# Tok2 steps between the halves of a channel unit, and the score rounds of batch 1 from its second head quad on in twos

## The chip, the cores and the metric

The kernel runs on one core of a Trainium2 chip. The metric is the device time of one execution in microseconds; the time before is 375.89 us, the median of six executions (374.99 to 380.59). All times below are microseconds unless marked otherwise. In the profile PE is TensorE (matmuls), PEld its weight loads, DVE VectorE, ACT ScalarE, POOL GpSimd, and SP SyncE, which here only issues transfers.

## What is computed

Sigmoid attention over 8 batches of 12 heads, 448 positions and 64 channels a head, and then one MLP-mixer block (token mixing over positions, channel mixing over the 768 features):

```python
scores = scale * q @ k.T - log(S)            # per batch and head, S = 448
attn   = 1 / (1 + exp(-scores))
x      = (attn @ v)  laid out as (8, 448, 768)
h      = relu(x.T @ w_tok1) @ w_tok2         # 448 -> 256 -> 448, per batch
u      = x + h.T
h2     = relu(u @ w_ch1) @ w_ch2             # 768 -> 1536 -> 768
out    = u + h2
```

All matmuls of the kernel are in fp16 with fp32 sums; inputs and output are fp32.

## The kernel before

Every piece of work is an `Op`: a name, an engine, an estimated duration, what must come before it, the buffers it uses, and a function that emits its instructions. `Plan.run` plays the whole kernel through by these estimates before anything is emitted: for each engine it picks the next operation, and where TensorE is free it asks `choose`. The operations are then emitted in the order of the planned starts. On the chip each engine works through its own list in that order, and waits where something that it needs is not there yet. So an edit of `choose` can move any step of the kernel, and with it the order on the other engines.

The steps of TensorE, with their names (b is the batch, m one of three head quads, four heads each):

- `S_b_m_i` is a score round, i = 0 to 6: four 64x64 matmuls of 448 columns that run side by side in the four quarters of the array (L578). It fills one of two score buffers in PSUM (`wide`). ScalarE then makes the sigmoid of it (`sig`, L594), which frees the buffer.
- `V_b_m` is the value step of a quad: 28 matmuls of 64x64 (L616) into two PSUM banks; ScalarE reads them out (`xT`, L653), and the result is laid back into `X` by a transpose on TensorE (`B_b_m`, L675) or, in most batches from 2 on, by a DMA transpose from SP (`x_b_m_s`, L664).
- `K1_b` (tok1, L817 and L857) and `K2_b_blk_half` (tok2, L933) are the two token matmuls. For batches 2 to 7 a part of them runs as 64x64 matmuls (`V1_b_t`, L841, and `V2_b`, L891; the code calls these tails). After tok2, VectorE forms u = x + h (L955, L923), ScalarE casts it to fp16 (L963), and it is turned into `uT`, by SP (`uT_b_blk`, L991) or, for the last two blocks of batches 1 and 2, on TensorE (`U_b_blk`, L976).
- `C1_b_cb` (channel 1, L1007, twelve units a batch) and `C2_b_blk_half` (channel 2, L1066, six or eight units) are the channel matmuls, 128x128. Each unit is planned in two halves, the second named with `_h`: 3 + 3 matmuls in a channel-1 unit, 6 + 6 in a channel-2 unit. Both halves sum into one PSUM bank; VectorE reads it out at the end (L1023 for channel 1, L1079 for channel 2).

There are four such banks (`bank`), shared by all steps but the scores. The loads of q, k and v come from POOL's queue and are held back by small copies on POOL (`gate`, L781), each of which waits for a sigmoid three head quads earlier. From batch 2 on k and q are permuted on POOL (L496) and transposed by SP (`turnk`, `turnq`, L501). SP also stores the results (`st_b_blk`, L1050 and L1044). SP's list is worked through in order, so a transfer that is not ready holds those behind it.

Score rounds come in `groups`, which are issued as one choice. For batch 1 each round is a group by itself (`parts`), with its three value steps as groups between them; from batch 2 on two rounds make a group, at times with a value step. `due` says from how much done mixer work on a group is due: -1 for batches 0 and 1 (always), and for later ones by LEAD and SPAN. `choose` collects the candidates that could start, keeps those within 0.06 us of the first, and takes the lowest priority number p:

- a due group has p = 1, one that is not due 5;
- tok1 and tok2 have 2, channel 1 has 3, channel 2 has 4;
- the first tok2 of a pair has 4.5 as long as less than REST of other mixer work was done since the last tok2; tok2 of batch 0 has 3.5;
- the second half of a channel unit has 1.2.

Of the kernel before, what the change touches and what calls it, by code (L numbers as in the profile page):

```python
# [55 lines left out]
class Plan:  # L56
# [15 lines left out]
    def op(self, name, engine, us, emit, after=(), uses=(), rank=0.0):  # L72
        o = Op(name, engine, us, emit, after, uses, rank)
        self.ops.append(o)
        return o
# [56 lines left out]
    def run(self, choose):  # L132

        lists = {}
        for o in self.ops:
            if o.engine != "PE":
                lists.setdefault(o.engine, []).append(o)
        free = dict.fromkeys([*lists, "PE", "POOL"], 0.7)
        free["POOL"] = 0.8
        mode = [None]  # L140
        self.left = len(self.ops)
        while self.left:
            best = None
            for e, ops in lists.items():
                if e == "LD":
                    ops = ops[:1]
                for o in ops:
                    r = self.ready(o)
                    if r is None:
                        continue  # L150
                    at = free[e]
                    if e == "LD":
                        at = max(free["POOL"], self.landed[-8])
                    key = (max(r, at), o.rank, r)
                    if best is None or key < best[0]:
                        best = (key, e, o)
            pick = choose(self, free["PE"])
            if pick is not None:
                t, ops, kind = pick
                if best is None or t <= best[0][0]:  # L160
                    for o in ops:
                        r = self.ready(o)
                        t = max(t, r, free["PE"])
                        if kind != mode[0]:
                            t += 0.1
                            mode[0] = kind
                        self.hold(o)
                        o.start, o.end = t, t + o.us
                        free["PE"] = t = o.end
                        self.log.append(o)  # L170
                        self.left -= 1
                    continue
            if best is None:
                raise RuntimeError(
                    "\n".join(
                        f"{o.name} <- {[d.name for d in o.after if d.end is None]}"
                        for o in self.ops
                        if o.start is None
                    )[:1500]
                )  # L180
            (t, _, _), e, o = best
            self.hold(o)
            o.start = t
            if e == "LD":
                far = self.load_far if self.pipe > 50.0 else 0.4
                free["POOL"] = t + o.n * o.issue
                self.pipe = max(self.pipe, free["POOL"] + 1.3) + o.us
                while self.hitch and self.pipe > self.hitch[0][0]:
                    self.pipe += self.hitch.pop(0)[1]
                o.end = self.pipe + far  # L190
                self.landed += [o.end] * o.n
            elif e == "SP":
                free[e] = t + o.us
                o.end = t + self.far + min(5.0, max(0.0, self.pipe - t - 0.5))
            else:
                o.end = free[e] = t + o.us
            lists[e].remove(o)
            self.log.append(o)
            self.left -= 1
        self.log.sort(key=lambda o: o.start)  # L200
        for o in self.log:
            o.emit()
# [3 lines left out]
def kernel(  # L206
# [23 lines left out]
    DH = D // 2  # L230
    att_scale = 1.0 / math.sqrt(E)
    att_bias = -math.log(S)
    LEAD, SPAN, REST, LATE = 20.0, 0.86, 0.8, 0
    FILL, UP, SURE = 21.0, 7, 0.8
    PACK, PACK2 = range(2, 8), range(2, 8)
    JOIN, PULL, ALONE = 0.05, 3.0, 3.5
    PAUSE = 1.5

    assert (B, H, S, E) == (8, 12, 448, 64) and D == 768 and TT == 256 and CC == 1536
# [178 lines left out]
    for x in ("q", "k"):  # L418
        o = next(early[(0, x)])
# [52 lines left out]
    def filler():  # L472


        spot = bank(f"fill_{fill['n']}", [128, 256])

        def emit():
            nc.tensor.matmul(
                out=spot[:, :], lhsT=uT[0][:, 0, 0:128], rhs=uT[0][:, 0, 0:256], start=True, stop=True
            )  # L480

        fill["n"] += 1
        return op(f"fill_{fill['n']}", "PE", 0.11, emit, [up], [spot, uT[0]])
# [292 lines left out]
    for n, unit in enumerate(units[6:], 6):  # L776
        for what, i in (("k", 1), ("q", 3), ("v", 5)):
            sig, at = rounds_of[units[n - 3]][i]
# [4 lines left out]
            o = op(f"gate_{what}_{n}", "POOL", 0.1, gate, [sig], [at, mark], rank=-5)  # L783
# [325 lines left out]
    for b in range(B):  # L1109
        rs = [o for o in visits[b] if o.name[0] == "S"]  # L1110
        vs = [o for o in visits[b] if o.name[0] == "V"]
        if b == 0:
            groups += [(b, i, [o]) for i, o in enumerate(rs)]
        else:
            if b == 1:
                parts = [[o] for o in rs]
                parts[9].append(vs[0])
                parts[15].append(vs[1])
                parts = [[o] for g in parts for o in g] + [[vs[2]]]
                groups += [(b, i / len(parts), g) for i, g in enumerate(parts)]  # L1120
                continue
            if b == 2:
                line = [(c, i / 21, o) for c in range(2, B) for i, o in enumerate(o for o in visits[c] if o.name[0] == "S")]
                value = [o for c in range(2, B) for o in visits[c] if o.name[0] == "V"]
                for i in range(0, len(line), 2):
                    part = [o for _, _, o in line[i : i + 2]]
                    if value and i >= 7 * (len(line) // 7 - len(value)) + 7 + LATE:
                        part.append(value.pop(0))
                    groups.append((*line[i][:2], part))
                groups += [(B - 1, 1.0, [o]) for o in value]  # L1130
    mix = [sum(o.us for o in (*K[b], *C1[b], *C2[b])) for b in range(B)]
    base = [sum(mix[:b]) for b in range(B)]
    state = {"done": 0.0, "chosen": None, "rest": 9.0}

    def due(g):
        b, i, _ = g
        return -1.0 if b < 2 else base[b - 1] - LEAD + i * SPAN * mix[b - 1]

    def settle():
# [6 lines left out]
        if any(o.name[:3] == "V2_" for o in c[2]):  # L1146
            state["rest"] = -PAUSE
        if row is not groups and c[2][0].name[0] != "V":
# [4 lines left out]
    def choose(plan, t):  # L1153
        settle()
        tails[:] = [o for o in tails if o.start is None]
        g = groups[0] if groups else None
# [9 lines left out]
        if groups:  # L1166
            g = groups[0]
            r = plan.ready(*g[2])
            if r is not None:
# [6 lines left out]
                p = -1 if g[0] == 0 else 1 if state["done"] >= due(g) - (PULL if more else 0) else 5  # L1176
# [9 lines left out]
        for rank, kinds in ((2, K), (3, C1), (4, C2)):  # L1186
            n = 0
            for row in kinds:
                for o in row:
                    if o.name[:2] == "K2" and o.name[-1] == "1" and row.index(o) > 0 and row[row.index(o) - 1].name[:-1] == o.name[:-1]:  # L1190
                        n += 1
                        continue
                    r = plan.ready(o)
                    if short and rank == 2:
                        r = None
                    if r is not None:
                        p = 4.5 if o.name[:2] == "K2" and o.name[-1] == "0" and state["rest"] < REST else rank
                        if o.name[:4] == "K2_0":
                            p = 3.5
                        if o.name[-2:] == "_h":  # L1200
                            p = 1.2
                        cands.append((max(r, t), p, [o], "128", row, o))
                    n += 1
                    if n > (3 if rank == 2 else 0):
                        break
                if n > (3 if rank == 2 else 0):
                    break
        o = fill.get("op")
# [5 lines left out]
        if 3.0 < t < FILL and (not cands or min(c[0] for c in cands) > t + 0.12) and up.start is not None:  # L1214
            if any(x <= t - SURE for x, _ in plan.free_slots("bank", up)):
                o = fill["op"] = filler()
# [11 lines left out]
    with tc.manual_schedule():  # L1228
        plan.run(choose)
# [30 lines left out]
```

## Time and profile before

| what | value |
|---|---|
| median of six executions | 375.89 us (374.99 to 380.59) |
| the profiled execution's own time | 374.99 us |
| its span, first to last instruction | 373.2 us |
| ScalarE sigmoids (L594) | 172, 987 ns each |
| channel 1 on TensorE (L1007) | 576 matmuls, 119.6 us busy |
| channel 2 on TensorE (L1066) | 672 matmuls, 117.1 us busy |
| scores (L578) and values (L616) on TensorE | 672 and 672 matmuls, 53.4 and 36.5 us busy |
| tok2 (L933) on TensorE | 104 matmuls, 21.6 us busy |
| transposes of u by SP (L991) | 24, 2.6 / 3.8 / 6.8 us to landing (least, median, most) |
| granted TensorE clock | 1.000 of full speed in the mean |

The page gives busy time for each engine as a share of the span, then the span in 40 slices with one digit each (the busy share in tenths). A timeline row has the start, the length, the engine, the line of the code, the operation and its count; "x4" means that four instructions in a row were merged. Matmuls overlap in the array, so their lengths are longer than the distance from one start to the next. Time in brackets at the end of a row is how long the engine had been idle, and what ended that.

### The profile page before, as it was taken

To read this page: it belongs to the slowest core of one execution; us is meant where nothing else is said; L and a number is where in the kernel's file an instruction comes from. 1 tells how busy PE (TensorE), PEld (TensorE's weight loads), DVE (VectorE), ACT (ScalarE), POOL (GpSimd) and SP (SyncE) were. 2 spreads that over 40 slices of the span, in tenths; PEclk is the share of its full clock that TensorE was granted. 3 is DMA by queue.
4 is the path that set the end of the run, shared out by engine and by line. 5 is a ranking of instruction groups with operands and counts; after the bars stand their busy time and mean duration, and the time that the engine had idled before them with its cause. 6 is when DMAs were issued, how large, how long until landed. Compare 5 with 4: busy or idle time off the path is not lost.

```text
span 373.2 us, 7967 instructions
## 1 busy us (share of the span) xinstructions
PE 365.0 (98%) x3188; PEld 186.3 (50%) x3188; DVE 175.5 (47%) x414; ACT 207.7 (56%) x269; POOL 115.4 (31%) x261
## 2 busy tenths in 40 slices
PE   8999999999999999999899999999999999999995
PEld 4455445554444544455444545444455555555653
DVE  4467336643424544343244454754462257665221
ACT  5996992377777767788567576845655121100000
POOL 8883326343453435444443343430000000000000
PEclk9999999999999999999999999999999999999999
DMA  6999999599999999999999899993104463300344
GB/s 101 180 185 206 210 209 180 115 186 191 120 138 141 198 159 126 131 137 191 205 182 133 127 185 198 166 160 73 30 2 113 95 135 87 74 0 2 84 103 110
DMA packets 97013, 50.06 MB, mean 134 GB/s; under 512 B 70544, under 2 KB 93456, under 8 KB 96976
## 3 DMA queue, kind: packets, MB, share of 16 engines
q0 software_dynamic: 24080, 21.62, 41.6%
q1 hardware_dynamic: 72656, 27.62, 41.5%
q8 instruction: 25, 0.41, 0.5%
q10 hardware_dynamic: 240, 0.31, 0.2%
q14 instruction: 12, 0.10, 0.1%
HBM read 43.45 MB, written 11.01 MB: 146 GB/s over the span
## 4 chain that ended last, share of the span: by engine, by line
PE 94%; DVE 1%; DMA 1%; ACT 1%; issue 0%; ACTq 0%
PE c L1007 30%; PE c L1066 29%; PE qk L578 11%; PE xa L616 8%; PE yn L933 5%; PE k L857 3%; DMA uT<-u 1%; PE tq L524 1%; PE tk L524 1%; PE xb L675 1%; PE idle L463 1%; ACT attn L594 1%; PE k L817 1%; PE k L841 1%; PE k L707 1%; PE yt L891 1%
## 5 line engine op out<-in xcount | busy, mean ns | idle before, releaser
L594 ACT ACTIVATE attn<-qk,att_bias 128x896 f16<-128x896 f32 (+1 forms) x172 | 161.5, 987 | 59.9 <-PE qk L578 59.0
L1007 PE MATMUL c<-uT,w_ch 128*128 128x448 f16 x576 | 119.6, 353 | 1.2 <-DMA uT<-u 1.2
L1066 PE MATMUL c<-w_ch,h2aT 128*128 128x384 f16 x576 | 100.0, 326 | 0.0
L1023 DVE TENSOR_SCALAR h2aT<-c 128x384 f16<-128x384 f32 x96 | 53.5, 557 | 80.4 <-PE c L1007 80.3
L1007 PEld LDWEIGHTS <-w_ch 128*128 128x128 f16 x576 | 52.5, 98 | 58.2 <-issue 13.4
L1066 PEld LDWEIGHTS <-h2aT 128*128 128x128 f16 x576 | 54.8, 98 | 40.6 <-issue 5.9
L1079 DVE TENSOR_TENSOR u<-u,c 128x384 f32<-128x384 f32 x48 | 26.6, 554 | 67.5 <-PE c L1066 67.2
L578 PE MATMUL qk<-qT,kT 64*64 64x448 f16 x672 | 53.4, 363 | 1.2 <-ACT qT L547 0.5
L616 PE MATMUL xa<-attn,v 64*64 64x448 f16 x672 | 36.5, 350 | 0.0
L781 POOL COPY mark<-attn 1x1 f16<-1x1 f16 x54 | 9.6, 178 | 80.3 <-ACT attn L594 78.3
L963 ACT ACTIVATE u<-u 128x768 f16<-128x768 f32 x21 | 17.7, 843 | 28.9 <-DVE u L955 28.9
L578 PEld LDWEIGHTS <-kT 64*64 64x64 f16 x672 | 14.6, 104 | 32.4 <-issue 29.9
L496 POOL COPY kp<-k 128x384 f16<-128x384 f16 (+1 forms) x54 | 21.2, 429 | 19.0 <-DMA k<-in_k_dram 15.0
L955 DVE TENSOR_TENSOR u<-x,yn 128x384 f32<-128x384 f16 x48 | 24.6, 548 | 4.8 <-PE yn L933 4.7
L653 ACT ACTIVATE xT<-xa 128x448 f16<-128x448 f32 (+2 forms) x61 | 22.2, 440 | 7.2 <-PE xa L616 5.7
L616 PEld LDWEIGHTS <-v 64*64 64x64 f16 x672 | 19.5, 107 | 11.8 <-issue 0.7
L496 POOL COPY qp<-q 128x384 f16<-128x384 f16 (+1 forms) x54 | 21.3, 431 | 12.4 <-DMA q<-in_q_dram 12.4
L933 PE MATMUL yn<-h,w_tok 128*128 128x384 f16 x104 | 21.6, 327 | 0.0
L1023 DVE TENSOR_SCALAR h2odd<-c 128x64 f16<-128x64 f32 x96 | 20.5, 214 | 0.0
L340 POOL DMA_DIRECT2D q<-in_q_dram x21 | 15.0, 716 | 7.5 <-issue 5.8
L1066 PE MATMUL c<-w_ch,h2odd 128*128 128x384 f16 x96 | 17.1, 327 | 0.0
L340 POOL DMA_DIRECT2D k<-in_k_dram x21 | 15.1, 721 | 4.5 <-issue 4.5
(73 smaller groups left out, 205.9 us busy)
## 6 DMA issues: line engine op xcount, KB each, us to landing
out_dram<-u SPq DMA_DIRECT2D x48, 192.0 KB, 3.0
k<-in_k_dram POOLq DMA_DIRECT2D x21, 224.0 KB, 5.3
q<-in_q_dram POOLq DMA_DIRECT2D x21, 224.0 KB, 5.4
v<-in_v_dram POOLq DMA_DIRECT2D x21, 224.0 KB, 5.5
w_ch<-in_moe_w_ch_dram POOLq DMA_DIRECT2D x6, 768.0 KB, 18.5
out_dram<-ut SPq DMA_DIRECT2D x6, 192.0 KB, 3.6
v<-in_v_dram POOLq DMA_DIRECT2D x6, 112.0 KB, 5.5
x<-xT SPq DMA_TRANSPOSE x32, 4.2
```

Source lines behind the costliest of these rows:

```text
L340: nc.gpsimd.dma_start(out=t.ap().rearrange("r h j e -> r h (j e)"), in_=heads.rearrange("(h s) (p j) e -> (s p) h (j e)", s=2, j=J),)
L496: nc.gpsimd.tensor_copy(out=pm[:, to, :, :], in_=src[:, fr, :, :])
L578: nc.tensor.matmul(out=ps[64 * s : 64 * s + 64, h, 0:S], lhsT=kT[64 * h : 64 * h + 64, i, s, :], rhs=qT[64 * h : 64 * h + 64, :, s, :], st ...
L594: nc.scalar.activation(out=at[:, hs, :], in_=ps[:, hs, 0:S], func=SIGMOID, bias=bias_t[:, :], scale=att_scale,)
L616: nc.tensor.matmul(out=ps[s](slice(64 * h, 64 * h + 64)), lhsT=vf[64 * s : 64 * s + 64, h, order[i], :], rhs=attn[i][64 * s : 64 * s + 64, ...
L653: nc.scalar.activation(out=xt[:, s, to : to + n], in_=ps[s](every)[:, fr : fr + n], func=COPYF)
L933: nc.tensor.matmul(out=ps[:, :], lhsT=w_tok2[:, t, s0 : s0 + 2, :], rhs=h1[b][:, t, c], start=(t == 0), stop=(t == 1),)
L955: nc.vector.tensor_tensor(out=to, in0=x, in1=y, op=ADD)
L1007: nc.tensor.matmul(out=ps[:, :], lhsT=w_ch1[cb // 4][:, db, 128 * (cb % 4) : 128 * (cb % 4) + 128], rhs=uT[b][:, db, :], start=(db == 0), ...
L1023: nc.vector.tensor_scalar(out=to, in0=ps[:, fr], scalar1=0.0, scalar2=None, op0=MAX)
L1066: nc.tensor.matmul(out=ps[:, :], lhsT=h, rhs=w, start=(cb == 0), stop=(cb == NCB - 1))
L1079: nc.vector.tensor_tensor(out=t, in0=t, in1=ps[:, :], op=ADD)
```

## The change

Two things are edited in `choose` and one in the making of `groups`; four constants change or are new. The second half of a channel unit goes from priority 1.2 to 2.1, behind tok1 and tok2 (2) and still ahead of any new unit (3 and 4). In batch 1 rounds 0 to 6 stay groups of one; rounds 7 to 20 become seven groups of two, and the value steps follow the groups that hold rounds 9 and 15. LEAD goes from 20 to 18, REST from 0.8 to 1.0, and the tok2 steps of batch 1 have a rest of their own, REST1 = 0. The text of an error message is shortened. No operation, buffer or transfer is added or removed.

```diff
-    LEAD, SPAN, REST, LATE = 20.0, 0.86, 0.8, 0
+    LEAD, SPAN, REST, LATE = 18.0, 0.86, 1.0, 0
     FILL, UP, SURE = 21.0, 7, 0.8
     PACK, PACK2 = range(2, 8), range(2, 8)
     JOIN, PULL, ALONE = 0.05, 3.0, 3.5
+    REST1 = 0
     PAUSE = 1.5
...
             if b == 1:
-                parts = [[o] for o in rs]
-                parts[9].append(vs[0])
-                parts[15].append(vs[1])
-                parts = [[o] for g in parts for o in g] + [[vs[2]]]
+                parts = [[o] for o in rs[:7]] + [rs[i : i + 2] for i in range(7, 21, 2)] + [[o] for o in rs[21:]]
+                for n, at in ((0, 9), (1, 15)):
+                    i = next(i for i, p in enumerate(parts) if rs[at] in p)
+                    parts.insert(i + 1, [vs[n]])
+                parts.append([vs[2]])
                 groups += [(b, i / len(parts), g) for i, g in enumerate(parts)]
                 continue
...
                     if r is not None:
-                        p = 4.5 if o.name[:2] == "K2" and o.name[-1] == "0" and state["rest"] < REST else rank
+                        p = 4.5 if o.name[:2] == "K2" and o.name[-1] == "0" and state["rest"] < (REST1 if o.name[:4] == "K2_1" else REST) else rank
                         if o.name[:4] == "K2_0":
                             p = 3.5
                         if o.name[-2:] == "_h":
-                            p = 1.2
+                            p = 2.1
                         cands.append((max(r, t), p, [o], "128", row, o))
```

More of the change, by code (lines that the diff above doesn't have):

```diff
@@ L178, in run @@
                         if o.start is None
-                    )[:1500]
+                    )[:200]
                 )
```

## The prediction, made before the result was known

> **What bounds the kernel now.** I read the page first, then the waits, then the TensorE timeline.
>
> ```profile
> span 373.2 us, 7967 instructions
> PE 365.0 (98%) x3188; PEld 186.3 (50%) x3188; DVE 175.5 (47%) x414; ACT 207.7 (56%) x269; POOL 115.4 (31%) x261
> ...
> ACT  5996992377777767788567576845655121100000
> ...
> PEclk9999999999999999999999999999999999999999
> ```
>
> TensorE is busy for 98% of the span at the full granted clock; no other engine passes 56%. The edit adds and removes no matmul, so the time can move only through what TensorE loses between matmuls: changes of tile mode, and waits. The first 100 TensorE steps of the two builds, up to `C1_0_1` at about 39 us, stand in the same order, and the last stages as well. The list of waits has one on a transfer:
>
> ```profile
> PE c L1007 <- DMA uT<-u: 1.2, 1, 1.2
> ```
>
> The prices are in the TensorE timeline: start, modelled busy time, instruction. I use distances between starts, since the ends are modelled.
>
> ```profile
> 46.16 0.38 PE L578 MATMUL qk<-qT,kT 64*64 64x448 f16 x4
> 46.48 0.74 PE L1007 MATMUL c<-uT,w_ch 128*128 128x448 f16 x3
> 47.15 0.38 PE L578 MATMUL qk<-qT,kT 64*64 64x448 f16 x4
> ...
> 90.80 0.57 PE L578 MATMUL qk<-qT,kT 64*64 64x448 f16 x8
> 91.31 2.44 PE L1007 MATMUL c<-uT,w_ch 128*128 128x448 f16 x12
> 93.68 0.57 PE L578 MATMUL qk<-qT,kT 64*64 64x448 f16 x8
> ```
>
> ```profile
> 317.92 24.00 PE L1007 MATMUL c<-uT,w_ch 128*128 128x448 f16 x126
> 341.76 23.56 PE L1066 MATMUL c<-w_ch,h2aT 128*128 128x384 f16 x144
> 365.16 4.06 PE L1066 MATMUL c<-w_ch,h2odd 128*128 128x384 f16 x24
> ```
>
> The last fence gives bare rates: 23.84 / 126 = 0.189 us for a channel-1 matmul, 23.40 / 144 = 0.1625 for a channel-2 one. A score round is four 64x64 matmuls of 448 columns side by side, in the time of one: 0.19 us. A value step is seven such fours, 1.33 us. The first fence shows rounds one at a time: 0.99 us from score to score, of which 3 x 0.189 + 0.19 is work, so 0.23 us is lost on the way into the 64x64 mode and out again. Rounds in twos: 2.88 us, less 12 x 0.189 and 2 x 0.19, leaves 0.23 too. The loss is per stretch in that mode, not per round.
>
> **Part 1, score rounds in twos.** I counted stretches of 64x64 steps in the two orders. Batch 1 falls from 19 to 15: rounds 0 to 6 stay single, the other fourteen become seven pairs, and some singles had already stood beside each other or a value step. The new planner constants (LEAD, REST, REST1) move steps in batches 3 to 7: one stretch fewer in batch 3, one more in batch 6. In all 111 become 107: 4 x 0.23 = **0.94 us saved**.
>
> A pair hands ScalarE two sigmoids at once, 0.95 us each (four in a row took 3.70), and fills both score buffers. In the new order four channel-1 halves stand between most pairs of batch 1: 2.88 us from pair to pair, against 1.90 of ScalarE. Where a value step stands there, it is two pair rounds, 1.33 of values, two halves and 0.23: 3.07 us, against 1.90 + 0.98 for its two reads. ScalarE keeps up, by only 0.2 us at the tightest. The nearest row to a failure is four rounds within 2.5 us at 103 to 105.5, which cost 0.32 us of idle TensorE on `attn`; that place stands unchanged in the new order. So I take 0 here, bounds 0 and 0.3 for each of two tight places.
>
> The Trainium skill, TensorEngine Tiling (Array Packing), section PSUM Bottleneck, speaks against pairs: tiling speeds up TensorE but not the reading of PSUM, which may become the limit. The rows above put the two side by side and the reading still fits. The same page's Key Properties say that changing the tiling mode drains TensorE, without a price. TensorE: Matmul & The Clock Gate, section Single matmul latency, has 166 ns as the constant of a lone matmul at full clock; as an estimate, two drains a stretch would make four stretches worth 1.33 us instead of 0.94.
>
> **Part 2, tok2 steps between the halves of a channel unit.** The second half's priority falls behind tok2 (1.2 to 2.1 against 2), so in 12 units one to three tok2 steps now stand between the halves (in three of them beside a score pair and a value step). Both are 128x128, so this costs no change of mode: 0 by itself. It holds the unit's bank for longer (0.65 us for two tok2 steps), and there are four banks. I walked the new order, adding start distances, and found one place where a bank comes late. In the new order V_1_2, K2_0_2_1, K2_0_3_0 follow each other, and K2_0_3_0 takes the bank that ScalarE still reads for V_1_2. The rows of the same value step now:
>
> ```profile
> 57.49 1.52 PE L616 MATMUL xa<-attn,v 64*64 64x448 f16 x28
> ...
> 59.06 0.98 ACT L653 ACTIVATE xT<-xa 128x448 f16<-128x448 f32 x2 [2.18 <-PE xa L616]
> ```
>
> The first read (0.54 us of the two) ends 2.11 us after the value step starts, and the hand-over takes 0.05; K2_0_3_0 could start at 1.45 + 0.33 = 1.78. **Lost: 0.4 us** (bounds 0, if its bank is another, and 0.6 with the tok2 step behind it). What is queued behind it is all of TensorE.
>
> **Part 3, the wait for uT.** This is C1_3_0, the first step of channel 1 in batch 3, waiting for the last of four transposes:
>
> ```profile
> 180.65 0.57 PE L578 MATMUL qk<-qT,kT 64*64 64x448 f16 x8
> 182.43 2.44 PE L1007 MATMUL c<-uT,w_ch 128*128 128x448 f16 x12 [1.21 <-DMA uT<-u]
> ```
>
> ```profile
> 175.29 1.86 SPq L501 DMA_TRANSPOSE kT<-kp  x1
> 177.25 1.29 SPq L991 DMA_TRANSPOSE uT<-u  x1
> ```
>
> A pair before a 128-row step takes 0.51, so C1_3_0 could have started at 181.16; it lost 1.27. The tok2 step that feeds this transpose, K2_3_2_1, started at 171.84 (second of the two at 171.51). From there: 2.3 us to the end of the cast (174.13), 3.1 in SP's queue behind two transposes and a store, 5.14 to land. TensorE had 9.32 us of work between. In the new order it has K2_3_2_1 0.33, eight channel-2 halves 8 x 0.975, six rounds 1.14, a value step 1.33, three stretches 0.70: 11.3 us, two halves more. The same chain needs 10.55, so **the wait of 1.27 us goes**, with 0.7 to spare. SP's queue ahead of this transpose changes: x_4_1_0, x_4_1_1 and turnq_5_1 in place of uT_3_1 and turnk_5_2. uT transposes landed in 2.6 to 6.8 us; at 6.8 the new wait is about 1.0, so the bounds are a gain of 1.27 and of 0.3. What is late next: nothing that I find. The same distance at batches 4 and 5 grows by 1 and 2 us, at batch 6 it shrinks by some 0.7 where about 3.9 was spare (landed 308.2, used 312.1), and batch 2 is unchanged. The store st_2_2 moves from before turnk_6_0 to behind x_5_1_1; the u buffer it frees is wanted by batch 4's sums 7.3 us after C2_2_2_1's second half, against 0.55 for the add, 1.2 of issue and 3.0 to land. The gates of batch 2's loads follow batch 1's later sigmoids, but its transposes have at least 3.7 us to spare.
>
> **The sum.** 0.94 + 1.27 - 0.4 = 1.8 us less. The profiled execution took 374.99 (span 373.2 and 1.8 around it), the lowest of six; the median is 0.9 above it. So 373.2 for an execution like the profiled one, and 375.89 - 1.8 = **374.1** as the median, 0.5% less.
>
> **Rivals.** *The wait stays*: the new SP order or the loads beside it delay the transpose, and C1_3_0 waits as long as before. For: transposes issued beside loads landed in 5 to 7 us here, late ones without loads in 2.6. Then 0.54 is saved: 375.3.
> *More than that goes*: the median's 0.9 us over the profiled run is more of the same wait, since nothing else on TensorE hangs on a transfer. Then 373.2. Against: start-up waits on loads too.
> *Slower*: the last transpose of uT of batch 3 gets stuck in SP's queue. The three transposes put ahead of it took 1.8, 2.26 and 1.25 us of SP in this run; with 5.3 in the queue and 6.8 to land it is there 14.4 us after K2_3_2_1, a wait of 3.1: net 1.3 slower, 377.2. It decides from 13.1 us on, as then the wait eats all that is saved; 1% slower needs 16.9.
> *The change doesn't do what it says*: excluded by the order for the tok2 steps, but pairs save only four stretches where seven pairs suggest seven.
>
> **How the numbers follow.** Forecast 0.66 (its own range 373.5 to 374.7), wait stays 0.12, more goes 0.10, stuck transpose 0.10, something not seen 0.02. One per cent, 3.76 us, is about what a measurement tells from no change. Faster by that would need 372.1, but all that TensorE can win here is 0.94 + 1.27 + 0.9 = 3.1: 0.05. Slower by that needs 5.6 us of new waits: 0.07. Within: 0.88. The range takes in 372.8 (all 3.1 gone) and 376.3 (half of the stuck case).
>
> **What would show it.** Right: no idle TensorE before C1_3_0; 107 stretches; score pairs of batch 1 at 2.88 us distance; an idle time of 0.4 us on tok2 (L934 in the new file) near 64 us, ended by ScalarE's reading of `xa`. Wrong: a wait on `uT` at any batch's first channel-1 step, waits of score rounds on `attn` in batch 1, or a new wait of the sums on an output transfer near 210 us.

## The result, and the profile after

The changed kernel takes 373.71 us in the median (373.25 to 374.88, 20 executions); the kernel before, over 41 executions, 376.55. The ratio is 0.9918, with a 95% interval of 0.9899 to 0.9937: 0.6 to 1.0% faster. The profiled execution took 373.39 us, its span 371.6; before it was 374.99 and 373.2. So two differences have to be explained: 1.6 us between the two profiles, which were to differ by 1.8, and some 3 us between the medians, which were to differ by 1.8 too.

The page of the changed kernel (its lines are one higher than before from L237 on; in the runs below they are up to three higher):

```profile
span 371.6 us, 7967 instructions
PE 364.5 (98%) x3188; PEld 186.2 (50%) x3188; DVE 176.6 (48%) x414; ACT 207.6 (56%) x269; POOL 115.6 (31%) x261
...
L934 PE MATMUL yn<-h,w_tok 128*128 128x384 f16 x104 | 21.7, 327 | 0.2 <-ACT xT L654 0.2
```

The number of instructions is the same and the busy share of TensorE too: busy time does not show this change. The last line shows the wait that tok2 had not had before.

TensorE's timeline of the changed kernel in batch 1 (start, modelled length, instruction):

```profile
40.62 0.57 PE L579 MATMUL qk<-qT,kT 64*64 64x448 f16 x8
41.12 2.44 PE L1008 MATMUL c<-uT,w_ch 128*128 128x448 f16 x12
43.50 0.57 PE L579 MATMUL qk<-qT,kT 64*64 64x448 f16 x8
```

A pair of rounds with four channel-1 halves behind it, 2.88 from pair to pair, with no wait on ScalarE. The stretches of 64x64 work are 107 where they were 111, and the distances between starts fit 0.23 us for each, as before.

The first channel-1 step of batch 3 in the changed kernel, on TensorE, and then SP's queue before it:

```profile
175.28 0.57 PE L579 MATMUL qk<-qT,kT 64*64 64x448 f16 x8
175.69 1.49 PE L617 MATMUL xa<-attn,v 64*64 64x448 f16 x28
177.11 1.31 PE L1008 MATMUL c<-uT,w_ch 128*128 128x448 f16 x6
```

```profile
166.90 2.89 SPq L665 DMA_TRANSPOSE x<-xT  x2
169.88 1.38 SPq L992 DMA_TRANSPOSE uT<-u  x1
171.35 1.18 SPq L1051 DMA_DIRECT2D out_dram<-u  x2
```

The step starts 1.42 after the value step, which is its 1.33 and the way out of the mode: nothing is waited for. The transpose was issued at 169.88 and landed 4.42 later, at 174.3, so 2.8 us were to spare.

Two waits are new. In TensorE's timeline the tok2 step behind the value step of batch 1 (63.58) is followed by the next only at 64.29, 0.71 later where 0.335 is usual:

```profile
62.13 1.52 PE L617 MATMUL xa<-attn,v 64*64 64x448 f16 x28
63.58 0.50 PE L934 MATMUL yn<-h,w_tok 128*128 128x384 f16 x2
64.29 0.92 PE L934 MATMUL yn<-h,w_tok 128*128 128x384 f16 x4 [0.21 <-ACT xT L654]
```

and one more 0.11 is lost inside the four matmuls at 64.29, where a bank waits for VectorE. The other is near 233, in the timeline of all engines, on a weight load of channel 1 in batch 4:

```profile
232.66 0.56 DVE L924 TENSOR_TENSOR ut<-ut,yt 64x384 f32<-64x384 f32 x1
...
233.26 0.30 PEld L1008 LDWEIGHTS <-w_ch 128*128 128x128 f16 x3 [0.56 <-DVE ut L924]
```

There the unit takes a bank that VectorE's sums of batch 5's tail still read. From start to start it costs 0.29.

The account of the two profiles from the distances between starts: four stretches fewer, -0.92; the wait for uT of batch 3, -1.28; the tok2 wait, +0.48; the wait behind batch 5's tail, +0.29; and the changed kernel's execution came to its first channel-1 step 0.20 earlier (36.84 against 37.04), in a part that both kernels have in common. The sum is -1.63, and the last TensorE step started 1.62 earlier. Nothing is left over.

### The profile page after: what moved, and what is told of

Same layout as the page of the kernel before. It is cut to its first block, busy times and chain, and to the rows that moved or that the text cites. A ratio compares the mean times of both kernels' runs of the same rounds, so it can differ in the third digit from the quotient of the medians.

```text
span 371.6 us, 7967 instructions
## 1 busy us (share of the span) xinstructions
PE 364.5 (98%) x3188; PEld 186.2 (50%) x3188; DVE 176.6 (48%) x414; ACT 207.6 (56%) x269; POOL 115.6 (31%) x261
## 4 chain that ended last, share of the span: by engine, by line
PE 92%; POOL 3%; DMA 2%; DVE 1%; ACT 1%; issue 1%; DVEq 0%; ACTq 0%; POOLq 0%
PE c L1067 30%; PE c L1008 29%; PE qk L579 11%; PE xa L617 8%; PE yn L934 5%; PE k L858 4%; DMA w_tok_s<-in_moe_w_tok_dram 2%; POOL k L330 1%; POOL q L330 1%; PE xb L676 1%; PE k L818 1%; PE k L842 1%; PE k L708 1%; PE yt L892 1%; ACT attn L595 1%
## 5 line engine op out<-in xcount | busy, mean ns | idle before, releaser
L1008 PE MATMUL c<-uT,w_ch 128*128 128x448 f16 x576 | 118.2, 353 | 0.1
L579 PE MATMUL qk<-qT,kT 64*64 64x448 f16 x672 | 52.2, 363 | 1.1 <-ACT qT L548 0.4
L871 DVE TENSOR_SCALAR h<-k 128x384 f16<-128x384 f32 x24 | 12.7, 557 | 9.8 <-PE k L858 9.8
```

What stands on the lines that cost most here:

```text
L579: nc.tensor.matmul(out=ps[64 * s : 64 * s + 64, h, 0:S], lhsT=kT[64 * h : 64 * h + 64, i, s, :], rhs=qT[64 * h : 64 * h + 64, :, s, :], st ...
L1008: nc.tensor.matmul(out=ps[:, :], lhsT=w_ch1[cb // 4][:, db, 128 * (cb % 4) : 128 * (cb % 4) + 128], rhs=uT[b][:, db, :], start=(db == 0), ...
```

## The experiments

### Where do the other 1.2 us of the median come from?

The kernel before has times from 374.8 to 383.0; the changed kernel 373.25 to 375.9. Theory A puts the spread on the wait for uT of batch 3, theory B on the start. The kernel before was profiled in five more executions (look1 to look5, the kernel unchanged), and one pair of transfers in SP's queue was exchanged, in each direction.

**look1, look2.**

> The kernel before, looked at in another execution. Theory A: what spreads the times of the kernel before (374.99 to some 378) is how long the first channel-1 step of batch 3 waits for the last transpose of u. Then this execution's time is 373.7 plus that wait: 375.0 with a wait of 1.3, 376.5 with one of 2.8. Theory B: the spread comes from the first 37 us, where TensorE waits for the first loads. Then the wait is near 1.3 whatever the time is, and the first channel-1 step of batch 0 starts later than 37.0 by what the time is over 375.0.

> A second such look, with the same expectations: theory A has time = 373.7 + the wait for uT of batch 3; theory B has the wait at 1.3 and the start of batch 0's first channel-1 step moved by the rest.

| execution of the kernel before | time | first channel-1 step of batch 0 | wait for uT of batch 3 |
|---|---|---|---|
| first profile | 374.99 | 37.04 | 1.28 |
| look1 | 375.53 | 37.28 | 1.55 |
| look2 | 377.02 | 38.38 | 1.93 |
| look3 | 375.46 | 37.23 | 1.56 |
| look4 | 374.90 | 37.16 | 1.04 |
| look5 | 374.89 | 37.05 | 1.16 |

The wait is counted from start to start, as in the prediction. Both move. Of look2's 2.03 us over the first profile 1.34 arise at the start and 0.65 in the wait. Its TensorE timeline shows the late load:

```profile
13.39 0.55 PE L616 MATMUL xa<-attn,v 64*64 64x448 f16 x8
15.27 0.41 PE L524 MATMUL tk<-ident,k 128*64 128x128 f16 x8 [1.33 <-DMA k<-in_k_dram]
```

So neither theory holds alone. In these executions the granted clock was full until TensorE's last matmul; where their mean is below 1 (0.997 in look3), it fell only behind that. The executions of 377.65 and more were not among them.

**swap_sp**: the kernel before, with two entries of SP's queue exchanged.

```diff
+        by = {o.name: o for o in self.log}
+        by["turnk_5_2"].start = by["uT_3_2"].start + 0.001
         self.log.sort(key=lambda o: o.start)
```

> The kernel before with one exchange in SP's queue: the last transpose of u of batch 3 goes ahead of the transpose of k for head quad (5,2), which stood before it. TensorE's order is that of before. The transpose is issued some 1.9 us earlier (175.3 in place of 177.25), which is more than the wait of 1.27. Both theories: no wait at batch 3's first channel-1 step, profiled span 1.3 less (371.9). Theory A: nearly all of the spread goes with it, median near 373.9, ratio 0.992 to 0.994, times within 1 us of each other. Theory B: median 1.3 less than before, ratio 0.9965, and the spread of several us stays.

Median 374.08 (373.59 to 375.36, 12 executions), ratio 0.994 (0.9909 to 0.9971). The median and the narrow spread are A's, yet the profile shows a wait still, in TensorE's timeline and in SP's:

```profile
180.52 0.57 PE L580 MATMUL qk<-qT,kT 64*64 64x448 f16 x8
182.00 2.25 PE L1009 MATMUL c<-uT,w_ch 128*128 128x448 f16 x11 [0.91 <-DMA uT<-u]
```

```profile
174.30 3.22 SPq L993 DMA_TRANSPOSE uT<-u  x2
177.63 2.23 SPq L503 DMA_TRANSPOSE kT<-kp  x1
```

The transpose was issued at 175.66 as meant, 1.6 earlier than before, but took 6.30 to land where it had taken 5.14. Most of what the queue gave, the transfer took back: the wait is 0.98. That a wait shorter by some 0.3 narrows the spread from 8 us to 2 fits neither theory. It points to something that a wait sets off.

**late_ut**: the changed kernel with the opposite exchange.

```diff
+        by["uT_3_2"].start = by["turnk_5_2"].start + 0.001
```

> The changed kernel with the opposite exchange: the last transpose of u of batch 3 goes behind the store and the transpose of k for head quad (5,2). It is then issued near 174.2 in place of 169.9 and lands at 178.5 to 180.5, where batch 3's first channel-1 step could start at 177.1: a wait of 1.4 to 3.4. Theory A: the median rises by about as much, to 375.1 to 377.1, and the times spread over 2 us or more as those of before do. Theory B: the median rises by the wait, the spread stays as narrow as that of the changed kernel (373.25 to 374.88).

Median 375.49 (374.94 to 379.02), ratio to before 0.9976 (0.9936 to 1.0017). TensorE's timeline has a wait of 1.73 at this step, from start to start:

```profile
176.48 1.49 PE L619 MATMUL xa<-attn,v 64*64 64x448 f16 x28
179.63 1.29 PE L1010 MATMUL c<-uT,w_ch 128*128 128x448 f16 x6 [1.66 <-DMA uT<-u]
```

The profiled span is 2.5 longer than the changed kernel's: 1.73 of it is this wait, and the other 0.79 was there already at the first channel-1 step of batch 0 (37.63 against 36.84). The median rose by 1.78. This one wait, put back, takes more than half of the 2.84 between the medians away, and times of 378.45 and 379.02 came back.

### Does the wait lower TensorE's clock?

Most executions come with their mean granted clock, 1 being full speed; for the kernel before these are the 64 that ran beside the experiments, for the changed kernel two more than its median counts. In the kernel before 25 of 64 have 0.995 or less, and these took 377.65 to 383.02; of the other 39, all but three (377.48, 378.22 and 380.49) are between 374.77 and 376.84. In the changed kernel it is 2 of 22, in swap_sp none of 12, in late_ut 2 of 12 (376.45 and 379.02; its 378.45 has 0.999). So some long times have another cause than the clock. None of these was profiled, and that cause stays open. Theory C says that the wait, where it is long enough, lowers the clock behind it. Theory D says that the clock falls for other reasons.

**late_ut2**: the transpose further behind.

```diff
+        by["uT_3_2"].start = by["turnq_5_2"].start + 0.001
```

> The changed kernel with the last transpose of u of batch 3 put further behind, after the transpose of q for head quad (5,2). It is issued near 178 and lands at 182 to 184; batch 3's first channel-1 step could start at 177.1, so it waits 5 to 7. Theory C: a wait of TensorE that is long enough lowers its clock, and this is why half of the executions before are slow (their mean granted clock is 0.990 to 0.995 where the quick ones have 0.998 to 1.000). Then most executions of this kernel have a mean clock of 0.995 or less, the profile shows a stretch at half the clock right behind the wait, and the time is 373.7 + 5 to 7 + 2 to 4. Theory D: the lower clock has nothing to do with that wait (it comes at the start or at random). Then the clock is 0.998 or more in about as many executions as with the changed kernel (20 of 22), and the time is 373.7 + 5 to 7, that is 378.7 to 380.7.

Median 380.87 (379.54 to 382.95), ratio 1.0098 (1.0057 to 1.0138). All ten executions have a mean clock of 0.995 or less. The timeline of TensorE, and the busy time and clock by stretches (the column after POOL is the granted clock):

```profile
176.09 1.49 PE L619 MATMUL xa<-attn,v 64*64 64x448 f16 x28
182.32 2.40 PE L1010 MATMUL c<-uT,w_ch 128*128 128x448 f16 x6 [4.74 <-DMA uT<-u]
184.65 0.96 PE L581 MATMUL qk<-qT,kT 64*64 64x448 f16 x8
185.54 4.36 PE L1010 MATMUL c<-uT,w_ch 128*128 128x448 f16 x15
189.83 0.57 PE L581 MATMUL qk<-qT,kT 64*64 64x448 f16 x8
```

```profile
177.00:181.40 4.40, 0.58 (x16) 0.12 (x4) 0.00 (x0) 1.96 (x5) 0.90 (x2) 1.00 1.18 225
181.40:188.40 7.00, 6.08 (x22) 2.11 (x23) 1.09 (x3) 1.91 (x2) 1.70 (x4) 0.51 0.44 48
188.40:196.00 7.60, 7.60 (x76) 3.44 (x76) 3.04 (x10) 4.74 (x7) 3.02 (x9) 1.00 0.65 90
```

The wait is 4.81. While it still lasts the granted clock falls to a half, for 6.83 us (181.49 to 188.32). Six channel-1 matmuls and the way out take 2.33 (182.32 to 184.65) where they take 1.24 at full speed. The slow stretch adds 2.8 to the 4.8. Theory D falls for this kernel: it had foreseen few lowered clocks, and there are ten of ten.

**look3, look4, look5** were to show such a stretch in the kernel before itself.

> The kernel before, another execution. Theory C (a wait of TensorE lowers its clock in some executions): if the mean clock is 0.995 or less, the time is 377.5 or more, and the half-clock stretch of 3.4 or 6.8 begins within 4 behind the end of the wait at batch 3's first channel-1 step (near 182 to 185); the matmuls there take twice as long. If the clock is 0.998 or more, the time is 375.0 to 376.5. Theory D: a lowered clock stands elsewhere, at the start or at no wait.

> The same once more: theory C puts a half-clock stretch, if there is one, right behind batch 3's wait for uT; theory D elsewhere.

> The kernel before, a last execution. Theory C: if the mean clock is 0.995 or less, the half-clock stretch begins within 4 behind the wait at batch 3's first channel-1 step and the time is 377.5 or more; at 0.997 or more it is 375.0 plus what the wait exceeds 1.3 and the start is late. Theory D: a lowered clock stands elsewhere.

None of the three was such an execution (374.89 to 375.46, clock 0.997 to 1.000). So for the kernel before the place of the lowered clock was not seen in a profile. It is inferred from late_ut2, where a much longer wait at the same step brings it. The waits that were seen there in the kernel before (1.04 to 1.93) left the clock up.

### Which part of the change does it?

**pairs_only**: the kernel before with the new `parts` of batch 1 alone.

> The kernel before with the score rounds of batch 1 in twos, and nothing else of the change. Theory A (stretches at 0.23 each, plus waits): 108 stretches in place of 111, 0.7 less; but tok2 of batch 3 stays where it was (9.3 of TensorE work between its last step and the first use of uT), so the wait of 1.3 to 1.9 stays, the bank wait of 0.5 near 64 appears, and a transpose of u of batch 1 on TensorE comes only 0.9 behind its last tok2 step, a wait of 1 to 2. Together no gain: 375.5 to 377. Rival: the pairs are what the change gains by, 373.9 to 374.5.

Median 375.78 (375.03 to 380.51), ratio 0.999 (0.9952 to 1.0029): no gain clear of the noise, as theory A had it. The profile fell on an execution with a lowered clock, and shows it at a much shorter wait (TensorE's timeline; the stretch from 88.9 to 92.4 below):

```profile
85.57 0.50 PE L933 MATMUL yn<-h,w_tok 128*128 128x384 f16 x2
87.58 0.51 PE L976 MATMUL ut<-ident,u_tail 128*128 128x128 f16 x6 [1.51 <-ACT u_tail L963]
...
88.61 0.38 PE L578 MATMUL qk<-qT,kT 64*64 64x448 f16 x4 [0.21 <-ACT attn L594]
88.93 4.11 PE L1007 MATMUL c<-uT,w_ch 128*128 128x448 f16 x12
92.97 0.57 PE L578 MATMUL qk<-qT,kT 64*64 64x448 f16 x8
```

```profile
88.90:92.40 3.50, 3.50 (x14) 1.47 (x11) 0.69 (x2) 1.53 (x2) 1.98 (x5) 0.51 1.16 159
```

Waits of 1.68 and 0.38 (start to start), then 3.41 us at half the clock: twelve channel-1 matmuls take 4.04 in place of 2.38. This costs as much again as the wait before it. By the mean clock it happened in 3 of 10 executions; the 380.51, at a clock of 1.000, is none of them. The wait at batch 3, which theory A had kept, did not occur in this one: the tok2 step that feeds the last transpose started 2.97 later than before (174.81 against 171.84), the transpose was issued only 1.12 later (178.37 against 177.25). So in this execution new waits, and not that one, take the gain away.

**no_pairs**: the changed kernel with the rounds of batch 1 one at a time.

> The changed kernel with the score rounds of batch 1 one at a time, as before; the priority of second halves and the constants are those of the change. Theory A: 111 stretches, so nothing of the 0.94; 11.3 of TensorE work between the last tok2 step of batch 3 and the first use of uT, so no wait there (1.3 less than before); the bank wait at 64 is gone, small waits of tok2 of batch 1 on VectorE come (0.1 each, some five), and 0.8 at the first channel-1 step of batch 1. 0 to 0.5 less than before in a profiled span, 374.5 to 375.2 in quick executions; and few executions with a lowered clock. Rival (pairs bring it all): 375.5 or more.

Median 374.04 (373.8 to 377.17), ratio 0.9927 (0.9893 to 0.9961), the clock lowered in one of 8. So without any pair in batch 1 most of the gain is there. The profile has no wait for uT at all. The waits of tok2 of batch 1 on VectorE are there (0.06 to 0.14, five, 0.61 together); the one foreseen at batch 1's first channel-1 step is not. Put back, the pairs are worth 0.33 in the median. They save 0.92 and the 0.61 of these waits; but the place where they put the last value step costs 0.48, and with them come the score wait of 0.49 near 104, which before and the changed kernel have and this one has not, and some 0.2 more behind batch 5's tail.

**no_const**: the changed kernel with its three constants put back: LEAD and REST as before, REST1 equal to REST.

> The changed kernel with LEAD, REST as before (20, 0.8) and REST1 equal to REST. Theory A: 108 stretches, 0.7 less than before; batch 3 has 11.4 of work behind its tail's second step, hardly a wait; but batch 4 has only 10.0 where before had 11.8, a wait for uT of 1 to 2.5 there, and a channel-2 step of batch 1 waits about 1.2 for a bank that VectorE's sums of batch 2's tail hold. 375.5 to 377.5, no gain. Rival: the constants do little, 373.7 to 374.3 as the change.

Median 376.87 (375.51 to 379.17), ratio 0.9998 (0.9962 to 1.0033). The waits are where they were foreseen: 1.20 at a channel-2 step of batch 1, and at the first channel-1 step of batch 4, in TensorE's timeline:

```profile
226.63 2.11 PE L1067 MATMUL c<-w_ch,h2aT 128*128 128x384 f16 x12
231.64 2.62 PE L1008 MATMUL c<-uT,w_ch 128*128 128x448 f16 x13 [2.90 <-issue]
```

From start to start this lost 3.06, more than the 2.5 given. At batch 3 this kernel waits for nothing: the priority and the pairs cure that wait without the constants, and open these two. The clock was not lowered in this execution, at a wait of 3.06, and in only one of ten by the mean. So the length of the wait alone does not decide it; the last section has what the traces show of that.

**best**: the changed kernel with three numbers changed.

```diff
-    LEAD, SPAN, REST, LATE = 18.0, 0.86, 1.0, 0
+    LEAD, SPAN, REST, LATE = 18.0, 0.84, 1.0, 0
...
-    REST1 = 0
+    REST1 = 0.8
...
-                parts = [[o] for o in rs[:7]] + [rs[i : i + 2] for i in range(7, 21, 2)] + [[o] for o in rs[21:]]
+                parts = [[o] for o in rs[:5]] + [rs[i : i + 2] for i in range(5, 21, 2)] + [[o] for o in rs[21:]]
```

> The changed kernel with SPAN 0.84, REST1 0.8 and the pairs of batch 1 from round 5 on. 105 stretches in place of 107: 0.46 less. Value step 2 of batch 1 no longer stands just before the tok2 steps that want its bank: 0.48 less. Two score pairs of batches 2 and 3 stand further apart: 0.49 less. The bank wait behind batch 5's tail (0.29) stays, and at the first channel-1 step of batch 1 there may be 0.1. Theory A: profiled span 1.3 less than the changed kernel's (370.2 to 370.5), 372.1 to 372.6 in the median, ratio to before 0.985 to 0.990, mean clock 0.998 or more in nearly all executions. Rival: the shorter distances bring a wait for uT of batch 1 of 1 or more, 373.5 to 375.5, and lowered clocks.

Median 372.33 (371.98 to 373.06), ratio to before 0.9896 (0.9857 to 0.9935), clock 0.998 or more in all six. The profiled span is 370.2, 1.4 less than the changed kernel's, which is what was expected of the two stretches (0.46), the tok2 wait (0.48) and the score wait (0.49). Behind the first channel-1 step, of the waits only the 0.29 behind batch 5's tail is left: the last value step of batch 1 is now followed by channel 2, and no tok2 step wants its bank.

```profile
62.94 1.52 PE L617 MATMUL xa<-attn,v 64*64 64x448 f16 x28
64.39 1.80 PE L1067 MATMUL c<-w_ch,h2aT 128*128 128x384 f16 x10
```

## Why the prediction was right, and where it was not

The median was given as 374.1, in a range of 372.8 to 376.3; it is 373.71. That the level came within 0.4 is partly luck. The six executions that it started from had a median of 375.89, the 41 have 376.55; from there the fall was 2.84, and not 1.8. Point by point:

- **The price of a stretch, 0.23.** Right: four fewer gave 0.92. Since the trace has a price for the way into the mode and out, the figure worked out from two drains (1.33 for four stretches) was not needed, and it is too high.
- **ScalarE keeps up with the pairs.** Right: no score round of batch 1 waits. The row that it took as nearest to a failure, at 105.5, had cost more than the 0.32 of idle time, 0.49 from start to start.
- **The bank of the last value step, 0.4 lost.** Right in place, 0.48 in size (0.37 and 0.11).
- **"I found one place where a bank comes late".** Wrong: there are two. The second is the channel-1 unit in batch 4 behind batch 5's tail, 0.29.
- **The wait for uT goes.** Right: 1.28 in the profile. It had 2.8 to spare instead of 0.7, since SP's queue took 1.5 in place of 3.1 and the landing 4.4 in place of 5.1, while the cast was done 0.3 later. Its reading that transposes landed in 5 to 7 us beside loads and in 2.6 without was coarse: in the profile of before the sixteen of u up to 246 us, where the last load is issued, took 2.8 to 6.8, the eight behind it 2.6 to 3.6.
- **The sum, 1.8 less.** Near for the profiles: 1.6, of which 0.2 is the start, so that the terms themselves gave 1.4, and the 0.29 that was missed is most of the difference. Near too for executions at full clock: the changed kernel's 20 with a mean clock above 0.995 have a median of 373.7, the 39 such executions of before 375.6.
- **The rival "more than that goes"** came nearer to the medians, with another mechanism than it gave. It took the excess of the median for a longer wait at the same step. The wait varies, from 1.04 to 1.93 in six executions, but that explains tenths. The mis-sized term is the wait's price: 1.27 was read from one execution at full clock, and where such a wait lowers the clock it costs another 1.7 (3.41 us at half speed) to 2.8 (6.83). In the kernel before, 25 of 64 executions have a clock that fits this. That part, for the kernel before itself, is inferred from late_ut2 and pairs_only, not seen.
- **Which part gains.** The prediction had it about evenly, 0.94 from the pairs and 1.27 from the wait, less 0.4 that the pairs lose. The runs have the pairs as 0.3 and the rest as most of it (no_pairs 0.9927). That rest needs the constants beside the priority: no_const (0.9998) loses the wait at batch 3 and gets two others. The constants without the priority were not run.

## What to carry to other kernels

On a kernel whose TensorE is always busy, count what lies between its matmuls: each change of tile mode has a fixed price that distances between starts give, and each wait can be foreseen by adding up the work between a producer's last step and its first user and comparing that with the measured chain. A wait on a transfer is worth more than its length in one good profile: look at the spread of the times and at the mean granted clock of each execution, for waits of some two microseconds may be paid twice. A reordering that only moves steps can cure one such wait and open another, so a part of a change that looks independent may gain nothing by itself (here the pairs), or only where another part closes what it opens (here the priority and the three constants).

## What the hardware showed unexpectedly

- The clock fell to half after waits of 1.68 and 0.38 close together (3.41 us long, beginning 1.4 after the first wait's end), and after 4.81 (6.83 long); it did not after 3.06 in one execution. The Trainium skill, TensorE: Matmul & The Clock Gate, section What's actually happening, gives at least one idle window of about 3.4 us as what lowers it. The lengths of the slow stretches agree with one and two such windows. That a whole window must be idle does not agree with pairs_only, which lost 2.06 of 3.41; the measurement decides.
- Where the wait falls matters. In these traces the granted clock changes only at whole multiples of 3.413 us from its first change: it was full for 177.49 and 191.15 in late_ut2 and for 81.92 and 283.31 in pairs_only, which is 52, 56, 24 and 83 times that. Such periods are the rows below, first of pairs_only, then of no_const, with the granted clock behind POOL:

```profile
85.53:88.94 3.41, 1.69 (x21) 0.71 (x17) 1.36 (x3) 3.34 (x6) 0.89 (x2) 1.00 1.09 185
88.94:92.35 3.41, 3.41 (x14) 1.41 (x11) 0.69 (x2) 1.49 (x2) 1.98 (x5) 0.50 1.17 160
...
226.53:229.94 3.41, 2.16 (x16) 1.15 (x12) 2.30 (x5) 2.35 (x5) 0.92 (x3) 1.00 0.83 121
229.94:233.36 3.42, 1.72 (x10) 0.93 (x11) 0.39 (x1) 0.00 (x0) 1.18 (x3) 1.00 1.27 237
```

The 2.06 of pairs_only lie within one period, and the next is at half speed. The 3.06 of no_const are cut in two by a boundary, 1.36 before it and 1.70 behind, and the clock stays up. So what fits these traces is the time lost within one period, with the limit between 1.70 and 2.06. By that the waits of 1.04 to 1.93 seen in the kernel before are mostly too short; as an estimate, its quickest execution with a lowered clock (377.65), less 1.7 for the slow stretch, is 1.0 above the profiled one with its wait of 1.28, so its wait would be some 2.2.

- Issuing the transpose 1.6 earlier in swap_sp made it land only 0.4 earlier (181.96 against 182.39). Its time to land grew by 1.2, with loads in flight beside it in both.
